# An offline order of 1,663 steps searched again, and every SBUF operand moved to a multiple of 128 bytes in its partition

## The chip, the core and the metric

The kernel runs on one core of one Trainium2 chip, in one launch. The metric is device time in microseconds, the median of several executions; lower is better. One profiled execution of the kernel before gives the rows below.

## The reference

Windowed attention, then two feed-forward blocks, all in float32:

```python
# q, k, v: 4 batches, 8 heads, 576 positions, 64 per head; window 64
attn = softmax(q @ k.T / 8 where 0 <= row - column < 64)      # rows sum to 1
x    = (attn @ v), heads side by side                          # 2304 x 512
h    = x @ w_in;  g = h * tanh(softplus(h)); x2 = g @ w_out    # 512 -> 2048 -> 512
h    = x2 @ w_in2                                              # 512 -> 1024
y    = h * softmax(h); z = (y - mean(y)) / sqrt(var(y) + 1e-6) * g_ln
out  = z @ w_out2                                              # 1024 -> 512
```

## The kernel before

Each float32 product is made of three TensorE passes over operands rounded to `fp32r` halves (`hi` and `lo`): hi·hi, hi·lo and lo·hi. The weights come as pairs of 32-bit words and are turned into float32 and then into halves on ACT and DVE. Tokens go in five groups of 512, 512, 512, 384 and 384.

The work has three stretches that overlap. Attention (`a_qk` to `a_xl`) makes `xt`, the halves of x, two blocks of 64 tokens at a time. The first feed-forward block (`pe_m1`, L950; `act_m`, L960; `g_h`, `g_l`; `pe_m2`, L984; `pe_m2l`, L995) runs over tiles of 128 hidden units. The second block works on tiles of 128 tokens: seven products of a Strassen-like scheme for `w_in2` (`b_p`, L1118), sums on DVE (`b_c`, L1133), softmax and norm (`b_max` to `b_z`), a transpose, and the last product (`b_m4`, L1235).

In `b_p` the stationary operand (`lhsT`) is `xs` for even pairs of token tiles and `xs_w` for odd pairs; the moving operand (`rhs`) is a half of `w_in2` in both. `xs` lies in a pool on the right side of SBUF, `xs_w` in the weights' pool on the left.

From attention block 16 on, and for every token tile of the second block, the transpose is not done on TensorE. DVE transposes blocks of 32 x 32 (`a_blocks`, L861; `b_tr`, L1200), one DMA writes them to DRAM (`blocks_out`, L375, tile `t_d`), and four DMAs read them back in the transposed order of blocks (`blocks_in`, L381). All DMAs are issued by SP, in program order.

The order of the instructions on every engine is not written out. `Schedule.run` simulates the kernel once while it is built: each step has a cost per engine, and of the steps that could start on an engine within `PATIENCE` (0.031 us) of the earliest, the one with the lowest entry in the list `RANK` is issued. `RANK` holds 1,663 numbers, found offline by a search over that same simulation. Behind a DMA step the simulation adds 1.6 us until what needs it may start, and 1.07 us between a step of another engine and a DMA that needs it. The costs are part of the program; the chip reads none of them, but they decide the order. Where the simulation foresees that TensorE idles in the first part, `bridge` issues matmuls of zeros (`zeros`, L693) to fill the time.

The rows of an SBUF tile begin where the pools before it end. On the left the pool `const` is first: `ident`, `mask_n` and `mask_0` of 512 bytes each per partition, starting at byte 1,152, then `g_sb` of 32 bytes; all other pools on the left follow, so each of their tiles (all halves of weights, `xt`, `g`, `lz`, `xs_w`) starts 32 bytes past a multiple of 128. The pools on the right are laid down from the top, which is such that `qk`, `v`, `s` and `xs` start 96 bytes past a multiple of 128.

Of the kernel before, what the change touches and what calls it, by code (L numbers as in the profile page):

```python
# [14 lines left out]
F32 = mybir.dt.float32  # L15
BF16 = mybir.dt.bfloat16
# [8 lines left out]
P = 128  # L25
# [4 lines left out]
N_T = 16  # L30
# [286 lines left out]
def attention_moe_solu(  # L317
# [46 lines left out]
    ident = const.tile([P, P], F32, name="ident")  # L364
    mask_n = const.tile([P, P], F32, name="mask_n")
    mask_0 = const.tile([P, P], F32, name="mask_0")
    g_sb = const.tile([P, NF2], F32, name="g_sb")

# [1298 lines left out]
```

## Time and profile before

| | us |
|---|---|
| median of 3 executions | 669.59 (665.54 to 669.97) |
| the profiled execution, its own time | 667.13 |
| span of its instructions | 665.4 |
| TensorE busy in the span | 649.1 (98%) |

The span runs from the first instruction to the last; the execution's own time has 1.7 us more around it. [...]

### The profile page before, as it was taken

The page shows a single profiled execution, that of the slowest core. Times are in us where ns is not written, and L with a number is a line of the kernel's source. Part 1 is how long each engine was busy: PE and PEld are TensorE (multiplying, and loading weights), DVE is VectorE, ACT ScalarE, POOL GpSimd, SP SyncE. Part 2 cuts the span into 40 slices and gives each one's busy share as a digit, 9 for nine tenths or more (in the row PEclk, how much of TensorE's full clock was granted, in tenths as well). Part 3 has the DMA queues.
Part 4 walks back from the last instruction along what each step waited for, and adds up shares of the span by engine and source line. Part 5 has one row for each costly group of instructions (what it writes and reads, how often), then busy time and mean ns, then how long its engine had stood idle before and what let it go on. Part 6 is the DMA issues. An engine that isn't in the chain of part 4 may idle for free.

```text
span 665.4 us, 10569 instructions
## 1 busy us (share of the span) xinstructions
PE 649.1 (98%) x4089; PEld 556.8 (84%) x4089; DVE 423.6 (64%) x741; ACT 348.3 (52%) x616; POOL 40.9 (6%) x63
## 2 busy tenths in 40 slices
PE   8899999999999989999999999999998999999997
PEld 6688888878888878788899999999886888788886
DVE  4778887876356656321115655776687988879751
ACT  5989775544344434232123545655576555657532
POOL 2412000000000001000000010000011001110100
PEclk9999999999999999999999999999999999999999
DMA  8874565576068453020044345602216555554562
GB/s 333 332 279 166 163 214 199 181 272 207 1 205 254 145 185 131 32 64 1 0 159 159 108 117 173 210 13 95 80 37 154 189 159 158 173 160 139 174 178 95
DMA packets 56962, 101.36 MB, mean 152 GB/s; under 512 B 5072, under 2 KB 30672, under 8 KB 56912
## 3 DMA queue, kind: packets, MB, share of 16 engines
q1 hardware_dynamic: 56912, 100.69, 46.5%
q8 instruction: 32, 0.52, 0.3%
q14 instruction: 18, 0.15, 0.1%
HBM read 74.45 MB, written 26.21 MB: 151 GB/s over the span
## 4 chain that ended last, share of the span: by engine, by line
PE 77%; DMA 10%; DVE 6%; ACT 3%; SPq 2%; issue 1%; POOL 0%; ACTq 0%; DVEq 0%
PE ps_h L950 26%; PE x L984 18%; PE po L1235 10%; PE x L995 9%; PE pb L1118 9%; DMA t_d<-s 3%; PE ps_o L903 2%; PE ps_s L741 2%; DMA h_b<-t_d 2%; DMA t_d<-y_b 2%; DMA st<-w_in 1%; SPq L381 1%; DMA room_q<-qk 1%; DMA pt<-t_d 1%; DMA xr<-x2d 1%
## 5 line engine op out<-in xcount | busy, mean ns | idle before, releaser
L950 PE MATMUL ps_h<-xt,w 128*128 128x512 f32 (+2 forms) x1008 | 205.4, 359 | 1.2 <-ACT mc L960 1.0
L950 PEld LDWEIGHTS ps_h<-xt,w 128*128 128x128 f32 x1008 | 177.2, 188 | 23.1 <-ACT mc L960 1.9
L984 PE MATMUL x<-g,w 128*128 128x512 f32 (+2 forms) x672 | 146.5, 359 | 1.0 <-DVE g L427 0.6
L984 PEld LDWEIGHTS x<-g,w 128*128 128x128 f32 x672 | 118.8, 188 | 16.3 <-ACT g L423 1.1
L443 DVE SCALAR_TENSOR_TENSOR g<-mc,g 128x512 fp32r<-128x512 f32 (+2 forms) x84 | 51.5, 618 | 94.8 <-ACT g L423 94.3
L1235 PE MATMUL po<-w,lz 128*128 128x512 f32 x432 | 101.4, 391 | 2.6 <-ACT lz L1215 2.5
L1235 PEld LDWEIGHTS po<-w,lz 128*128 128x128 f32 x432 | 80.6, 188 | 21.4 <-ACT lz L1215 4.6
L960 ACT ACTIVATE mc<-ps_h 128x512 f32<-128x512 f32 (+2 forms) x84 | 44.8, 535 | 98.5 <-PE ps_h L950 94.5
L995 PE MATMUL x<-g,w 128*128 128x512 f32 (+2 forms) x336 | 80.8, 362 | 0.0
L423 ACT ACTIVATE g<-mc 128x512 fp32r<-128x512 f32 (+2 forms) x68 | 39.2, 578 | 60.4 <-PE x L995 59.3
L995 PEld LDWEIGHTS x<-g,w 128*128 128x128 f32 x336 | 59.4, 188 | 7.9 <-issue 1.0
L1118 PE MATMUL pb<-w,xs 128*128 128x512 f32 x210 | 51.1, 395 | 0.0
L1118 PEld LDWEIGHTS pb<-w,xs 128*128 128x128 f32 x210 | 39.4, 188 | 9.2
L1118 PE MATMUL pb<-w,xs_w 128*128 128x512 f32 x168 | 39.8, 390 | 0.0
L1118 PEld LDWEIGHTS pb<-w,xs_w 128*128 128x128 f32 x168 | 31.5, 188 | 6.7
L1215 ACT ACTIVATE lz<-h_b 128x512 fp32r<-128x512 f32 x36 | 21.3, 626 | 29.6 <-DMA h_b<-t_d 19.4
L1219 DVE TENSOR_TENSOR lz<-h_b,lz 128x512 fp32r<-128x512 f32 x36 | 24.0, 686 | 17.3 <-ACT lz L1215 17.2
L508 DVE SCALAR_TENSOR_TENSOR st<-st 128x1024 uint32<-128x1024 uint32 x22 | 26.9, 1224 | 10.8 <-ACT st L493 9.2
L844 POOL TENSOR_TENSOR s<-s,rs 128x1024 f32<-128x1024 f32 x6 | 11.5, 1923 | 354.0 <-DMA x2d<-xs 187.3
L435 ACT ACTIVATE v_b<-pb 128x512 f32<-128x512 f32 x33 | 19.6, 595 | 20.0 <-PE pb L1118 18.2
L500 ACT ACTIVATE st<-st 128x1024 uint32<-128x1024 uint32 x22 | 25.4, 1156 | 6.3 <-DMA st<-w_out 6.3
L1150 ACT ACTIVATE e<-h_b,nm 128x1024 f32<-128x1024 f32 x18 | 20.7, 1151 | 9.1 <-DVE nm L1141 8.9
(133 smaller groups left out, 712.5 us busy)
## 6 DMA issues: line engine op xcount, KB each, us to landing
qk<-qk SPq DMA_DIRECT2D x32, 512.0 KB, 5.2
st<-w_out SPq DMA_DIRECT2D x12, 1024.0 KB, 5.7
st<-w_in SPq DMA_DIRECT2D x10, 1024.0 KB, 6.0
t_d<-y_b SPq DMA_DIRECT2D x18, 512.0 KB, 2.8
h_b<-t_d SPq DMA_DIRECT2D x72, 128.0 KB, 3.2
v<-v SPq DMA_DIRECT2D x32, 256.0 KB, 3.7
t_d<-s SPq DMA_DIRECT2D x10, 512.0 KB, 3.3
pt<-t_d SPq DMA_DIRECT2D x40, 128.0 KB, 3.1
```

Of the source, the lines that this page charges most:

```text
L423: nc.scalar.activation(out=hi, in_=x, func=ACTF.Copy, scale=1.0 if g is None else g)
L443: nc.vector.scalar_tensor_tensor(out=lo, in0=x, scalar=1.0 if g is None else g, in1=hi.bitcast(F32), op0=ALU.mult, op1=ALU.subtract)
L500: nc.scalar.activation(out=w, in_=w, func=ACTF.Copy, scale=0.9325 * 2.0**-29)
L508: nc.vector.scalar_tensor_tensor(out=lw, in0=uw, scalar=3, in1=lw, op0=ALU.logical_shift_left, op1=ALU.bitwise_or)
L950: nc.tensor.matmul(out=ps[:, :n], lhsT=w[:, a, k, fs], rhs=x[:, b, k, a0:a1], start=(idx == 0), stop=(idx == len(terms) - 1),)
L960: nc.scalar.activation(out=c[:, :n], in_=ht.pop(i)[:, :n], func=ACTF.Mish)
L984: nc.tensor.matmul(out=acc[j][m][:, a0:a1], lhsT=w[:, a, f % 4, m * P:(m + 1) * P], rhs=g[:, 0, :n], start=(i in opens and a == 0), stop=F ...
L995: nc.tensor.matmul(out=acc[j][m][:, a0:a1], lhsT=w[:, 0, f % 4, m * P:(m + 1) * P], rhs=g[:, 1, :n], start=False, stop=i in closes,)
L1118: nc.tensor.matmul(out=ps, lhsT=x[:, a, ix, k, :], rhs=w[:, k, :], start=first and n == 0, stop=n == len(terms) - 1, skip_group_check=not ...
L1215: nc.scalar.activation(out=lt[t][:, 0, fs].rearrange(SPLIT, i=4), in_=pst[t][:, :, fs], func=ACTF.Copy)
L1219: nc.vector.tensor_tensor(out=lt[t][:, 1, fs].rearrange(SPLIT, i=4), in0=pst[t][:, :, fs], in1=lt[t][:, 0, fs].bitcast(F32).rearrange(SPLI ...
L1235: nc.tensor.matmul(out=po[t], lhsT=lz[:, a, f, :], rhs=wt["w4", f // 4][:, b, f % 4, :], start=(c == 0 and idx == 0), stop=(c == 2 and idx ...
```

## The change

- `RANK` is replaced as a whole by another list, and twelve of the costs that the simulation uses are changed, up or down.
- `g_sb` leaves the pool `const` and gets a pool of its own behind the pools `st`, `x` and `m`; a pool `pad` of 96 bytes is laid down first on the right side. All operands of TensorE, and all other large tiles, then start at multiples of 128 bytes.
- The tile of zeros for `zeros` shrinks from 256 to 128 columns and is read twice as the moving operand; the matmuls stay 256 columns wide.

No operation is added or taken out; the order on every engine may differ.

```diff
 RANK = (
-    1391, 1126, 1485, 321, 317, 1647, 1410, 39, 308, 845, 739, 1366, 771, 176, 300, 796, 809, 70, 607, 668, 220, 44,
...
+    481, 441, 1200, 1017, 674, 1532, 1594, 90, 129, 446, 1432, 581, 510, 1398, 113, 784, 846, 1422, 1282, 1439, 29,
...
 )
...
-    g_sb = const.tile([P, NF2], F32, name="g_sb")
...
     m_p = actx.enter_context(tc.tile_pool(name="m", bufs=2))
+    g_p = actx.enter_context(tc.tile_pool(name="g_ln", bufs=1))
+    g_sb = g_p.tile([P, NF2], F32, name="g_sb")
...
+    pad = ctx.enter_context(tc.tile_pool(name="pad", bufs=1, side="right"))
+    pad.tile([P, 24], F32, name="pad")
...
-        w = sm_p.tile([P, 256], BF16, tag="warm", name="warm", bufs=1)
+        w = sm_p.tile([P, P], BF16, tag="warm", name="warm", bufs=1)
...
-            nc.tensor.matmul(out=ps[:, :256], lhsT=w[:, :P], rhs=w, start=True, stop=True)
+            nc.tensor.matmul(
+                out=ps[:, :256].rearrange("p (a b) -> p a b", a=2), lhsT=w, rhs=w.unsqueeze(1).to_broadcast([P, 2, P]),
+                start=True, stop=True,
+            )
...
-            r = step(dict(dve=0.35), t + offs[5], a_norm, n, after=[e1], new=[rs], uses=[nm, rs])
+            r = step(dict(dve=0.4), t + offs[5], a_norm, n, after=[e1], new=[rs], uses=[nm, rs])
...
-                sc = step(dict(dve=1.23 if n < N_T else 1.55), t + offs[1], a_scale, n, after=[qk, masks, mask_x] + moved[-1:], new=[s], uses=[S, s])
+                sc = step(dict(dve=1.23 if n < N_T else 1.42), t + offs[1], a_scale, n, after=[qk, masks, mask_x] + moved[-1:], new=[s], uses=[S, s])
...
-                bl = step(dict(dve=1.13), t + offs[7], a_blocks, n, after=[mu], uses=[s])
+                bl = step(dict(dve=1.25), t + offs[7], a_blocks, n, after=[mu], uses=[s])
...
-                mo = step(dict(dma=1.4), t + offs[8], a_out, n, after=[bl], new=[td, T], uses=[s, td])
-                c0 = step(dict(dma=2.0), t + offs[8], a_in, n, after=[mo], uses=[T, td])
+                mo = step(dict(dma=1.5), t + offs[8], a_out, n, after=[bl], new=[td, T], uses=[s, td])
+                c0 = step(dict(dma=2.6), t + offs[8], a_in, n, after=[mo], uses=[T, td])
...
-                q = step(dict(pe=1.362), a + P_AT[3], b_p, u, i, after=after, new=[bk[bank]] if first else [], uses=[bk[bank], xs_])
+                q = step(dict(pe=1.4), a + P_AT[3], b_p, u, i, after=after, new=[bk[bank]] if first else [], uses=[bk[bank], xs_])
...
-                    dict(dve=0.84), a + P_AT[5], b_c, u, i, c, after=after + [ob2], new=[hb[t]] if c == 0 else [],
+                    dict(dve=0.72), a + P_AT[5], b_c, u, i, c, after=after + [ob2], new=[hb[t]] if c == 0 else [],
...
-            sh = step(dict(dve=0.3), o[3], b_shift, t, after=[va], uses=[st])
+            sh = step(dict(dve=0.2), o[3], b_shift, t, after=[va], uses=[st])
...
-            tr = step(dict(dve=1.13), o[4], b_tr, t, after=[z, ob2], new=[Y], uses=[h, Y])
+            tr = step(dict(dve=1.25), o[4], b_tr, t, after=[z, ob2], new=[Y], uses=[h, Y])
...
-            mo = step(dict(dma=1.4), o[4], b_out_t, t, after=[tr], new=[td], uses=[Y, td])
-            mv = step(dict(dma=2.0), o[4], b_in_t, t, after=[mo], uses=[h, td])
+            mo = step(dict(dma=1.5), o[4], b_out_t, t, after=[tr], new=[td], uses=[Y, td])
+            mv = step(dict(dma=2.6), o[4], b_in_t, t, after=[mo], uses=[h, td])
```

## Rows read from the trace of the kernel before

**Rows 1.** The page's busy times and granted clock: us, share of the span, instructions.
```profile
PE 649.1 (98%) x4089; PEld 556.8 (84%) x4089; DVE 423.6 (64%) x741; ACT 348.3 (52%) x616; POOL 40.9 (6%) x63
...
PEclk9999999999999999999999999999999999999999
```
**Rows 2.** The page's chain that ended last, by engine.
```profile
PE 77%; DMA 10%; DVE 6%; ACT 3%; SPq 2%; issue 1%; POOL 0%; ACTq 0%; DVEq 0%
```
**Rows 3.** Stretches: length, PE, PEld, DVE, ACT, POOL busy; clock, DMA, GB/s.
```profile
0.00:20.00 20.00, 16.67 (x172) 13.10 (x172) 9.93 (x27) 12.65 (x59) 6.28 (x19) 1.00 0.92 343
...
200.00:250.00 50.00, 47.85 (x373) 39.12 (x372) 30.03 (x45) 20.25 (x26) 0.00 (x0) 1.00 0.62 195
...
500.00:550.00 50.00, 48.30 (x211) 38.88 (x210) 42.21 (x103) 29.23 (x52) 5.49 (x10) 1.00 0.58 163
550.00:600.00 50.00, 49.13 (x215) 39.85 (x214) 41.43 (x97) 29.30 (x54) 7.01 (x12) 1.00 0.51 159
```
**Rows 4.** TensorE's groups on `fp32r` halves: count, busy us, mean ns, idle before.
```profile
L950 PE MATMUL ps_h<-xt,w 128*128 128x512 f32 (+2 forms) x1008 | 205.4, 359 | 1.2 <-ACT mc L960 1.0
L984 PE MATMUL x<-g,w 128*128 128x512 f32 (+2 forms) x672 | 146.5, 359 | 1.0 <-DVE g L427 0.6 <-ACT g L423 0.4
L1235 PE MATMUL po<-w,lz 128*128 128x512 f32 x432 | 101.4, 391 | 2.6 <-ACT lz L1215 2.5
L995 PE MATMUL x<-g,w 128*128 128x512 f32 (+2 forms) x336 | 80.8, 362 | 0.0
L1118 PE MATMUL pb<-w,xs 128*128 128x512 f32 x210 | 51.1, 395 | 0.0
L1118 PE MATMUL pb<-w,xs_w 128*128 128x512 f32 x168 | 39.8, 390 | 0.0
```
**Rows 5.** TensorE's timeline, 531 to 546 us: start, length, first to last of a run.
```profile
531.24 11.04 PE L1235 MATMUL po<-w,lz 128*128 128x512 f32 x48
542.12 4.37 PE L1118 MATMUL pb<-w,xs 128*128 128x512 f32 x18
546.32 5.65 PE L1235 MATMUL po<-w,lz 128*128 128x512 f32 x24
```
**Rows 6.** Pieces of the chain on TensorE: start us, us, line, matmuls.
```profile
14.76 1.36 PE ps_s L693 x11
...
39.79 1.44 PE ps_h L950 x12
...
126.72 8.16 PE ps_h L950 x36
...
412.20 12.48 PE ps_h L950 x72
```
**Rows 7.** The group of the zeros between: their mean is the length of one.
```profile
L693 PE MATMUL ps_s<-warm 128*128 128x256 bf16 x20 | 2.5, 272 | 3.2 <-ACT s L435 1.6 <-ACT s L771 1.5
```
**Rows 8.** The chain around a block transpose of attention, 234 to 247 us.
```profile
234.55 1.16 DVE s L861
235.71 0.02 issue
235.72 5.79 DMA t_d<-s
...
242.85 3.10 DMA pt<-t_d
245.95 0.14 issue
246.09 1.15 PE ps_o L903 x32
```
**Rows 9.** The same of the second block, 556 to 567 us.
```profile
556.33 1.16 DVE y_b L1200
557.51 2.69 DMA t_d<-y_b
...
561.56 4.27 DMA h_b<-t_d
565.93 0.64 ACT lz L1215
566.61 3.48 PE po L1235 x14
```
**Rows 10.** The DVE transposes of blocks, by form.
```profile
L1200 DVE STREAM_TRANSPOSE y_b<-h_b 128x1024 f32<-128x1024 f32 x18 | 22.2, 1236 | 0.0
```
**Rows 11.** The first 100 us of L950, L984 and L995: PE, PEld, clock, DMA, GB/s.
```profile
0.00:100.00 100.00, 30.89 (x171) 25.82 (x172) 1.00 0.71 248
...
0.00:100.00 100.00, 17.25 (x96) 14.13 (x96) 1.00 0.71 248
...
0.00:100.00 100.00, 9.73 (x48) 7.31 (x48) 1.00 0.71 248
```

More of the change, by code (lines that the diff above doesn't have):

```diff
@@ L1420, in attend @@
                 sm = step(dict(dve=1.2), t + offs[5], a_sum, n, after=[ex], uses=[s])
-            r = step(dict(dve=0.35), t + offs[5], a_norm, n, after=[sm], new=[rs], uses=[rs])
+            r = step(dict(dve=0.4), t + offs[5], a_norm, n, after=[sm], new=[rs], uses=[rs])
             mu = step(COSTS["mul"], t + offs[6], a_mul, n, after=[r], uses=[s, rs], two=True)
```

158 rows, old and new, of the table RANK are left out of this document.

## The prediction

> **What bounds the kernel now.** I read the page's busy times first, then its chain, then TensorE's own spacing, then the stretches in which TensorE stands still. [...]
>
> That spacing is steady. 36 matmuls of 512 columns on `fp32r` halves take 8.16 us, 226.7 ns each; 72 of 384 take 12.48 us, 173.3 ns; 12 of 256 take 1.44 us, 120 ns [rows 6]. [...]
>
> One group is slower still. From 531.24 to 542.12 us 48 matmuls of `po` take 226.7 ns each; the next 18, whose stationary operand is `xs`, take 4.20 us, 233.3 ns; then `po` again [rows 5]. `xs_w` runs the same products from the left side. By the allocation, `xs` starts 96 bytes past a multiple of 128 and all the others 32, with the same kind of moving operand. So where an operand starts can matter: 6.6 ns per matmul between 96 and 32. What 0 gives, no row shows.
>
> **The change part by part.** The sum is made against the profiled execution's own 667.1 us (span 665.4 and 1.7 around it); the median of the runs shown is 669.6, 2.5 us more.
>
> *`xs` on a multiple of 128.* 210 matmuls [rows 4] at 6.6 ns is 1.4 us, if 0 is as good as 32. They lie in the last 180 us, where TensorE is the chain for most of the time, so I count all of it: -1.4 us. Left out if the place of `xs` is not the cause.
>
> *All other `fp32r` matmuls from 32 to 0.* They are 1008 + 672 + 432 + 336 + 168 = 2616 [rows 4]. [...] At worst 0 costs what 96 costs, +6.6 ns each, +17.3 us. I take 0. [...]
>
> [...]
>
> *The order.* TensorE's idle time that a changed cost can reach is where it waits for block transposes. From the end of the DVE transpose at 235.71 us to the product at 246.09 are 10.4 us [rows 8], and from 557.51 to 565.93 in the second block 8.4 us [rows 9]. The simulation before reckons 1.07 + 1.4 + 1.6 + 2.0 + 1.6 = 7.7 us for this way, the new one 1.07 + 1.5 + 1.6 + 2.6 + 1.6 = 8.4; the transpose itself goes from 1.13 to 1.25, where the trace has 1.24 [rows 10]. So the new order should start these ways about 0.8 us sooner, or put other matmuls in between. TensorE stands still 2.15 us in 200 to 250, 1.70 in 500 to 550 and 0.87 in 550 to 600 [rows 3]: 4.7 us. Moved 0.8 us sooner, the wait of 0.87 goes and the longer ones shrink; with something gained from sums that the old costs of `b_c` and `b_shift` made too long, I count -3 us. Bounds: -4.7 us, and +4, since the search knows neither the 10.4 us nor the slow reads beside full DMA queues and can put as much waiting elsewhere. The 3.3 us of idle time in the first 20 us [rows 3] sit beside DMAs at 92% and stay. The later pieces of a moved step go with it: a transpose moved forward takes five issues on SP with it, and SP's other loads stand behind them; loads are issued well ahead in the stretches from 200 us on, so I price that at nothing, and if it were not so the wait would be of the size of the +4. The cost 1.4 for `b_p` is a little too high if `xs` gets faster (63 steps by 0.04 us, 2.4 us over the last part); the order then has matmuls that end sooner than it thinks, which costs at most short waits on DVE.
>
> *The rest.* The zeros keep their 256 columns; `g_sb` is read by the same instructions; the smaller `memset` ends before the first loads have landed. Nothing.
>
> Sum: 667.1 - 1.4 - 0 - 3 = **662.7 us**; its own range, from the bounds of the order and of `xs`, is 658 to 669.
>
> **The rivals.**
>
> [...]
>
> [...] A stationary offset of 96 costs 6.6 ns more than 32; if 0 saves as much again, it is 2616 x 6.6 = 17.3 us and 210 x 13.2 = 2.8: 667.1 - 20.1 - 3 = 644 us, and up to 655 where the step is smaller (half of it, 3.3 ns).
>
> *The change does not do what it says.* The place of `xs` is not the cause (then all 210 stay at 233), and the new order's waits take the place of the old ones: 667 us, 664 to 671.
>
> *Slower.* 0 is as bad as 96: every `fp32r` matmul has the spacing that the rows of `xs` show, 233.3 ns for 512 columns. 667.1 + 17.3 - 3 = 681 us. It decides from the point where the loss passes 1% and what the order gives: (6.7 + 3) us / 2616 = 3.7 ns per matmul, all through the kernel. For it: offsets do matter in the trace. Against it: it needs 0 to be worse than 32, while 96 is worse than 32.
>
> **How the numbers follow.** Forecast 0.45, stream 0.22, half 0.15, no effect 0.10, slower 0.08. The predicted time is the forecast's, 662.7. To hold 8 in 10 the range reaches over the two fast rivals, down to 635, and up to 669; left out are the slower rival and some of the stream's and the no-effect case's spread. A measurement of this kernel tells about 1% from no change. Faster by over 1%: 0.22 + 0.15, and a quarter of the forecast where the order gives its upper bound, 0.48. Slower by over 1%: 0.08 and a little for a bad order, 0.09. Within 1%: 0.43.
>
> **What would show it.** [...] If `xs` stays at 233 while all start at multiples of 128, its place was not the cause. The idle time of TensorE in the two stretches after 200 us should fall from 4.7 to about 2 us; if it is as large at other places, the order gave nothing. I am wrong above all if the spacing of the 2616 changes.

## The result and the profile after

| | before | after |
|---|---|---|
| median, us | 668.49 (664.76 to 669.97, 6 runs) | 658.22 (656.25 to 659.02, 6 runs) |
| the profiled execution, us | 667.13 | 659.02 |
| span, us | 665.4 | 657.2 |

The ratio after to before is 0.9853, 95% interval 0.983 to 0.9875: 9.8 us less. The forecast of 662.7 was 4.4 us below the profiled execution of before; after's is 8.1 below it. The page of after, busy times, granted clock and chain, answers to [rows 1, 2]:

```profile
PE 645.9 (98%) x4080; PEld 556.7 (85%) x4080; DVE 424.3 (65%) x741; ACT 347.4 (53%) x617; POOL 47.7 (7%) x62
...
PEclk9899999999999999999999999999999999999999
...
PE 85%; DMA 8%; DVE 2%; ACT 1%; SPq 1%; issue 1%; POOL 0%; ACTq 0%
```

The span is 8.2 us shorter. Span less busy time is TensorE's standstill: 665.4 - 649.1 = 16.3 before, 657.2 - 645.9 = 11.3 after, 5.0 us less. The other 3.2 us are less busy time. Its groups, to be held against [rows 4]:

```profile
L1242 PE MATMUL po<-w,lz 128*128 128x512 f32 x432 | 100.8, 389 | 0.2 <-ACT lz L1222 0.2
...
L1125 PE MATMUL pb<-w,xs 128*128 128x512 f32 x210 | 49.9, 389 | 0.0
```

`xs` has lost 1.2 us of 51.1 and its matmuls now last as long as those of `po`; `po` has lost 0.6 of 101.4. Nine matmuls are gone (4089 to 4080): all are zeros, 59 before and 50 after, 1.0 us at (1360 - 272) / 10 = 108.8 ns from start to start [rows 6, 7]. The stretches that answer to [rows 3], with the same columns:

```profile
0.00:20.00 20.00, 16.38 (x174) 12.57 (x174) 11.60 (x28) 13.51 (x62) 9.17 (x20) 1.00 0.93 341
200.00:250.00 50.00, 48.84 (x387) 39.87 (x380) 31.04 (x47) 20.80 (x27) 0.00 (x0) 1.00 0.63 198
500.00:550.00 50.00, 49.76 (x219) 40.51 (x218) 44.63 (x109) 32.47 (x57) 8.11 (x10) 1.00 0.52 164
550.00:600.00 50.00, 50.00 (x222) 41.44 (x221) 43.35 (x105) 29.59 (x50) 11.69 (x14) 1.00 0.48 153
```

TensorE's standstill in the last three is 1.16, 0.24 and 0 us, where it was 2.15, 1.70 and 0.87. The chain around a block transpose of attention, then the first of the second block, against [rows 8, 9]:

```profile
216.71 4.08 DMA t_d<-s
222.13 5.25 DMA pt<-t_d
227.62 1.15 PE ps_o L910 x32
...
493.32 2.73 DMA t_d<-y_b
500.25 4.93 DMA h_b<-t_d
506.30 11.20 PE po L1242 x48
```

The second of the two DVE transposes there, from the timeline:

```profile
494.03 1.24 DVE L1207 STREAM_TRANSPOSE y_b<-h_b 128x1024 f32<-128x1024 f32 x1
```

The ways have not become shorter. From the first DMA's issue to the product it is 227.62 - 216.71 = 10.9 us in attention. In the second block the chain passes from one token tile to another on SP: the write at 493.32 us is the first tile's, while the product at 506.30 us reads the second tile's `lz`, whose transpose ended at 494.03 + 1.24 = 495.27. Its way is thus 11.0 us, where [rows 9] has 566.61 - 557.51 = 9.1. What is new is what TensorE has to do meanwhile: it works on other products, takes the second tile first, and waits 0.24 us for those 11.0.

### The profile page after: what moved, and what is told of

It is laid out like the page before. It is cut to its first block, busy times and chain, and to the rows that moved or that the text cites. A ratio compares the mean times of both kernels' runs of the same rounds, so it can differ in the third digit from the quotient of the medians.

```text
span 657.2 us, 10526 instructions
## 1 busy us (share of the span) xinstructions
PE 645.9 (98%) x4080; PEld 556.7 (85%) x4080; DVE 424.3 (65%) x741; ACT 347.4 (53%) x617; POOL 47.7 (7%) x62
## 4 chain that ended last, share of the span: by engine, by line
PE 85%; DMA 8%; DVE 2%; ACT 1%; SPq 1%; issue 1%; POOL 0%; ACTq 0%
PE ps_h L957 27%; PE x L991 17%; PE po L1242 15%; PE pb L1125 10%; PE x L1002 9%; PE ps_o L910 3%; DMA st<-w_out 2%; PE ps_s L748 2%; DMA room_q<-qk 1%; DMA st<-w_in 1%; PE ps_t L863 1%; DMA qk<-qk 1%; DMA pt<-t_d 1%; DMA h_b<-t_d 1%; SPq L380 1%
## 5 line engine op out<-in xcount | busy, mean ns | idle before, releaser
L1242 PE MATMUL po<-w,lz 128*128 128x512 f32 x432 | 100.8, 389 | 0.2 <-ACT lz L1222 0.2
L1125 PE MATMUL pb<-w,xs 128*128 128x512 f32 x210 | 49.9, 389 | 0.0
L1188 POOL TENSOR_SCALAR va<-va 128x1 f32<-128x1 f32 x18 | 12.2, 677 | 423.2 <-PE pb L1125 308.6
L1125 PE MATMUL pb<-w,xs_w 128*128 128x512 f32 x168 | 40.2, 390 | 0.0
L512 DVE SCALAR_TENSOR_TENSOR st<-st 128x1024 uint32<-128x1024 uint32 x22 | 28.5, 1297 | 10.9 <-ACT st L504 8.9
L1249 ACT ACTIVATE o<-po 128x512 f32<-128x512 f32 x18 | 10.7, 597 | 30.6 <-PE po L1242 17.1
L497 ACT ACTIVATE st<-st 128x1024 f32<-128x1024 f32 x18 | 20.7, 1151 | 11.5 <-DMA st<-w_in 9.8
```

Of the source, the lines that this page charges most:

```text
L497: nc.scalar.activation(out=w, in_=w, func=ACTF.Copy, scale=2.0**-112)
L512: nc.vector.scalar_tensor_tensor(out=lw, in0=uw, scalar=3, in1=lw, op0=ALU.logical_shift_left, op1=ALU.bitwise_or)
L1125: nc.tensor.matmul(out=ps, lhsT=x[:, a, ix, k, :], rhs=w[:, k, :], start=first and n == 0, stop=n == len(terms) - 1, skip_group_check=not ...
L1242: nc.tensor.matmul(out=po[t], lhsT=lz[:, a, f, :], rhs=wt["w4", f // 4][:, b, f % 4, :], start=(c == 0 and idx == 0), stop=(c == 2 and idx ...
```

## The experiments

**Layout alone, order alone.** One kernel has the layout part of the change (the smaller tile of zeros with it) and the list and costs of before; the other has the new list and costs with the layout of before.

```diff
-    g_sb = const.tile([P, NF2], F32, name="g_sb")
...
+    g_sb = g_p.tile([P, NF2], F32, name="g_sb")
...
+    pad.tile([P, 24], F32, name="pad")
```

> The kernel before with the new layout alone; its order and costs stay. Theory (the place of xs was the whole of the layout's part, the order the rest): xs falls from 233.3 to 226.7 ns, all other fp32r matmuls stay at 226.7, 173.3 and 120; 210 x 6.6 = 1.4 us less than before, ratio 0.998. Rival (aligned operands help elsewhere too, in transfers, DVE or ACT): 4 us or more less than before, ratio 0.994 or lower.

> The changed kernel with the layout of before: new list, new costs, old places. Theory: xs back at 233.3 ns; 1.4 us over the changed kernel's 658.2, so 659.6, ratio to before 0.987; TensorE idle as in the changed kernel, some 11 us. Rival (the layout carries more than xs): 662 or more, ratio over 0.990.

Layout alone: 665.37 us, ratio 0.9962 (0.994 to 0.9983). Order alone: 658.56 us, ratio 0.988 (0.9852 to 0.9909). Of the whole, then, some 2.5 us (1.1 to 4.0) are the layout's, and 7 to 8 the order's: 0.9853 / 0.9962 = 0.989 with the new layout, 0.988 with the old one. The profiled span of layout alone is 664.0, 1.4 us below before, and its `xs` group has 49.8 us. TensorE's stretches with the order alone (length, busy, clock, DMA, GB/s):

```profile
0.00:100.00 100.00, 94.72 (x943) 1.00 0.73 258
100.00:200.00 100.00, 99.96 (x601) 1.00 0.52 173
200.00:250.00 50.00, 49.77 (x382) 1.00 0.65 201
...
500.00:550.00 50.00, 50.00 (x220) 1.00 0.51 158
550.00:600.00 50.00, 50.00 (x220) 1.00 0.50 157
```

From 100 us to its last matmul TensorE hardly stops any more: 0.27 us in place of 5.1. In the first 100 us it stands still 5.28 us in place of 7.44.

**Is it the multiple of 128?** Five kernels keep the new order and move the left side, `xs`, or both. The distance below counts from the start of the moving half of the weight to the start of `xs`, within 256 bytes; in the kernel before it is 64.

```diff
+    const.tile([P, 24], F32, name="pad_l")
...
-    pad.tile([P, 24], F32, name="pad")
```

> The changed kernel with every operand 96 bytes past a multiple of 128, left and right. Theory A (what counts is how far the stationary operand's start stands from the moving one's within 128 bytes): all at 226.7 ns, xs too, and the time of the changed kernel, 658. Theory B (what counts is the start of the operand itself, and 96 is a slow place): 233 ns for 512 columns everywhere, 2826 x 6.6 = 18.7 us more, 677.

Here all operands start 96 bytes past a multiple of 128, as `xs` alone did before. The other four have a pad of 64 bytes on the left, or 32, 64 or 224 in place of 96 bytes on the right.

```diff
+    const.tile([P, 16], F32, name="pad_l")
```

> The changed kernel with all tiles of the left side 64 bytes past a multiple of 128 and xs on one. Theory A (distance of the two starts): xs at about 233 ns, since its weights stand 64 bytes away as they did before; all others at 226.7; 1.4 us over the changed kernel, 660. Theory B (own start): xs at 226.7 or less, the others between 226.7 and 233, so up to 9 us more, 660 to 667.

```diff
-    pad.tile([P, 24], F32, name="pad")
+    pad.tile([P, 8], F32, name="pad")
```

> The changed kernel with the left side on multiples of 128 and xs 64 bytes past one. Theory A (distance): xs at 233 ns as before, since the distance is 64 as before; others 226.7; 660. Theory B (own start, worse the further it stands from the multiple): xs between 226.7 and 233, some 230 ns; 659.

```diff
-    pad.tile([P, 24], F32, name="pad")
+    pad.tile([P, 56], F32, name="pad")
```

> The changed kernel with xs 128 bytes further down, still on a multiple of 128 but at a distance of 128 instead of 0 within 256 bytes from its moving operand. If 128 bytes are the unit, xs stays at 226.7 ns and the time at 658; if the unit is 256 bytes, xs is slower, like the 228.9 and 233.3 ns of the distances 192 and 64, and the time 0.5 to 1.4 us longer.

```diff
-    pad.tile([P, 24], F32, name="pad")
+    pad.tile([P, 16], F32, name="pad")
```

> The changed kernel with xs 32 bytes ahead of its moving operands. Theory A (distance within 256 bytes): between the 226.7 ns of 0 and the 233.3 ns of 64, so 227 to 233, and 658 to 660. Rival (own start): 226.7, since 32 was a fast place before.

The order is the same in all, so the same two runs of `xs` can be read from TensorE's timeline: one of 42 matmuls and one of 6. After:

```profile
487.89 9.68 PE L1125 MATMUL pb<-w,xs 128*128 128x512 f32 x42
...
540.91 1.52 PE L1125 MATMUL pb<-w,xs 128*128 128x512 f32 x6
```

The same place for `xs_w`, in the kernel after too:

```profile
478.37 9.68 PE L1125 MATMUL pb<-w,xs_w 128*128 128x512 f32 x42
```

All at 96:

```profile
486.27 9.68 PE L1124 MATMUL pb<-w,xs 128*128 128x512 f32 x42
...
539.28 1.52 PE L1124 MATMUL pb<-w,xs 128*128 128x512 f32 x6
```

64 on the left, `xs` on a multiple of 128:

```profile
485.57 9.78 PE L1126 MATMUL pb<-w,xs 128*128 128x512 f32 x42
...
538.23 1.54 PE L1126 MATMUL pb<-w,xs 128*128 128x512 f32 x6
```

All on multiples of 128, but `xs` 128 bytes further:

```profile
486.11 9.92 PE L1125 MATMUL pb<-w,xs 128*128 128x512 f32 x42
...
539.06 1.56 PE L1125 MATMUL pb<-w,xs 128*128 128x512 f32 x6
```

`xs` at 64, and at 32 (9.96 and 1.56 in both):

```profile
488.21 9.96 PE L1125 MATMUL pb<-w,xs 128*128 128x512 f32 x42
...
541.64 1.56 PE L1125 MATMUL pb<-w,xs 128*128 128x512 f32 x6
```

In these views a matmul lasts longer than it is to the start of the next (389 ns in the mean for `xs` in after), so that two in a row overlap. The difference of two runs leaves out the last one's length, and divided by 36 it is the time from start to start, the spacing: (9.68 - 1.52) / 36 = 226.7 ns, and so on.

| layout | distance within 256 | spacing of `xs`, ns | us |
|---|---|---|---|
| after | 0 | 226.7 | 658.22 (6 runs) |
| all at 96 | 0 | 226.7 | 657.72 (2) |
| `xs` at 32 | 32 | 233.3 | 659.83 (1) |
| `xs` at 64 | 64 | 233.3 | 660.62 (1) |
| `xs` 128 further | 128 | 232.2 | 657.89 (1) |
| left at 64 | 192 | 228.9 | 656.59 (1) |

A multiple of 128 is not needed (all at 96 is as fast as after; ratio to before 0.9841, 0.9812 to 0.9869) and not enough (128 further is on a multiple and slow). In these kernels it went by whether both operands of a matmul start at the same place within 256 bytes: 226.7 ns where they do, 228.9 to 233.3 where they don't. With 64 on the left `xs` stands where it stands in after, and yet is slower, so that its own place is not the cause. The unit is not 512 either: by the allocation `xs` stands 256 of 512 bytes from its moving operand in after and `xs_w` 0, and both have 9.68 us for 42. The times of single runs can't rank layouts whose whole effect is 1.4 us; the spacings can. The expectation that took 128 as the unit fell with the kernel at 128, and 64 on the left gave 228.9 ns where it said 233.

**The same for the other operands.** 128 unused bytes ahead of the pool of `xt` and `g` put these moving operands 128 bytes from their stationary weights. All start on multiples of 128, as after.

```diff
     st_p = actx.enter_context(tc.tile_pool(name="st", bufs=2))
+    gap = actx.enter_context(tc.tile_pool(name="gap", bufs=1))
+    gap.tile([P, 32], F32, name="gap")
     x_p = actx.enter_context(tc.tile_pool(name="x", bufs=2))
```

> The changed kernel with 128 unused bytes laid ahead of xt and g: every operand is still on a multiple of 128, but the moving operands of the first feed-forward block now stand 128 bytes from their stationary ones within 256. Theory A (the distance of the two starts within 256 bytes sets the spacing, on any tile): the 2016 matmuls of that block go from 226.7, 173.3 and 120 ns to some 6 ns more, as xs did with a distance of 128 (232.6 ns); 12 us more, 670; po and pb unchanged. Rival (only the place of xs on the right side is slow): all as in the changed kernel, 658.

664.18 us, ratio 0.9938 (0.9916 to 0.996), 6 us slower than after. The timeline of this kernel, 512 and then 384 columns:

```profile
125.65 5.73 PE L959 MATMUL ps_h<-xt,w 128*128 128x512 f32 x24
...
136.81 14.09 PE L959 MATMUL ps_h<-xt,w 128*128 128x512 f32 x60
...
415.37 4.38 PE L959 MATMUL ps_h<-xt,w 128*128 128x384 f32 x24
...
421.69 12.80 PE L959 MATMUL ps_h<-xt,w 128*128 128x384 f32 x72
```

And of after:

```profile
125.08 5.60 PE L957 MATMUL ps_h<-xt,w 128*128 128x512 f32 x24
...
135.96 13.76 PE L957 MATMUL ps_h<-xt,w 128*128 128x512 f32 x60
...
410.54 4.32 PE L957 MATMUL ps_h<-xt,w 128*128 128x384 f32 x24
...
416.78 12.64 PE L957 MATMUL ps_h<-xt,w 128*128 128x384 f32 x72
```

512 columns: (14.09 - 5.73) / 36 = 232.2 ns against 226.7; 384 columns: 8.42 / 48 = 175.4 against 173.3. So the distance matters for the matmuls of the first block too, and costs 5.5 ns at 512 columns and 2.1 at 384. Twice as much time was expected, as if each of the 2016 paid alike. The groups of `ps_h` and `x` grow by 3.4 + 2.5 + 1.2 = 7.1 us of busy time. By these prices 1056 matmuls of 512 columns and 768 of 384 would make 5.8 + 1.6 = 7.4 us (an estimate), so that the 192 of 256 columns show none; `po` and `pb`, which were not moved, keep 100.8, 49.9 and 40.2.

**Where the order gains: early, late, or both.** Two kernels with the new layout run a fixed list of steps: those that start before 340 us in the simulation of one order, then the rest in the other's.

```diff
-            s.key = RANK[n]
...
+        seq = list(zip(SEQ, ENG))
...
+            for n, (s, e) in enumerate(todo):
```

> The changed layout; the steps that the simulation starts before 340 us in the new order, the rest in the order of before. TensorE idle before 340 us should be as with the new order (some 5.5 us), behind it as with the old one (3 us). Theory C (the gain of the order lies where TensorE stood waiting, 2.2 us in the first 100, 1.9 in 200 to 250, 3 behind 340, each worth its idle time): 665.4 of the layout alone less 4.1 to 5, 661. Rival D (the first part's gain is swallowed later, only the second block's part counts): 664 to 665.

> The reverse: the old order before 340 us, the new one behind it, changed layout. Theory C: 665.4 less the 3 us of waits behind 340 us and about 1 us of slower restarts after them, 661.5; both halves together then make up the order's 7 to 8 us. Rival D: all of the order's gain lies here, 658 to 659.

New early: 662.52 us, 0.9913 (0.9887 to 0.9938). New late: 663.06 us, 0.9929 (0.9909 to 0.9949). Against layout alone (0.9962) that is -3.3 and -2.2 us, each good to some 2 us by the intervals, and together 5.5 of the 7.3 that the whole new order gives there. TensorE's stretches in layout alone:

```profile
200.00:250.00 50.00, 47.86 (x373) 1.00 0.61 192
500.00:550.00 50.00, 48.04 (x205) 0.97 0.56 167
```

New early:

```profile
200.00:250.00 50.00, 50.00 (x389) 1.00 0.67 200
...
500.00:550.00 50.00, 48.50 (x214) 1.00 0.51 155
550.00:600.00 50.00, 48.41 (x214) 1.00 0.53 173
```

New late:

```profile
200.00:250.00 50.00, 47.71 (x372) 1.00 0.60 192
...
500.00:550.00 50.00, 48.91 (x214) 1.00 0.52 159
550.00:600.00 50.00, 50.00 (x222) 1.00 0.47 148
```

Layout alone stands still 2.14 us in 200 to 250 and 1.99 in 500 to 600. New early removes the first and has 3.09 in the second; new late keeps 2.29 in the first and has 1.09 in the second. Each half thus shortens the standstill of its own stretches only: the gain is not one event, and of what is removed early at most 1.1 us is given back late. The missing 1.8 us sit where the halves are joined, or within the intervals; which, these runs don't tell.

**Was it the way of the block transposes?** Layout alone, old order, but the DMAs of the second block's token tiles write and read only the first 64 of 256 elements.

```diff
-        nc.sync.dma_start(out=d.rearrange("i a b x -> (i a) b x"), in_=src.rearrange("p b h c -> p b (h c)"))
+        w = 64 if isinstance(key, tuple) else 256
+        nc.sync.dma_start(out=d.rearrange("i a b x -> (i a) b x")[:, :, :w], in_=src.rearrange("p b h c -> p b (h c)")[:, :, :w])
...
```

> The order of before with the changed layout; the transposes of the token tiles write and read only the first 64 of each 256 elements, so that the output is not the reference's. Theory (the old order's waits in the second block come from a way of the transposes that is longer than it reckoned): if the way gets shorter by 0.8 us or more, TensorE's idle time in 500 to 600 us falls from 2.0 to under 0.5 us, and the time by 2 us against the layout alone, to 663. Rival (the waits come from DVE being late, not from the way): the idle time stays near 2 us and the time at 665.

661.92 us, 0.9918 (0.9891 to 0.9944): 2.9 us below layout alone. The DMA issues of layout alone (count, KB, us from issue to landing):

```profile
t_d<-y_b SPq DMA_DIRECT2D x18, 512.0 KB, 2.9
h_b<-t_d SPq DMA_DIRECT2D x72, 128.0 KB, 3.0
```

And of the short way:

```profile
t_d<-y_b SPq DMA_DIRECT2D x18, 128.0 KB, 2.3
h_b<-t_d SPq DMA_DIRECT2D x72, 32.0 KB, 1.9
```

The way is 1.7 us shorter, and the stop in the second block goes with it. Layout alone, TensorE's timeline, then its stretches of 2 us:

```profile
506.94 9.18 PE L1242 MATMUL po<-w,lz 128*128 128x512 f32 x32 [1.96 <-ACT lz L1222]
...
508.00:510.00 2.00, 2.00 (x7) 0.60 0.37 80
510.00:512.00 2.00, 2.00 (x6) 0.55 0.00 0
```

The short way:

```profile
506.86 7.49 PE L1244 MATMUL po<-w,lz 128*128 128x512 f32 x32
```

So the old order's late waits were for this way, as the prediction had it. This kernel shortens the landing and relieves the DMA queues at once; the two weren't told apart.

**New costs with the old list.**

```diff
-                c0 = step(dict(dma=2.0), t + offs[8], a_in, n, after=[mo], uses=[T, td])
+                c0 = step(dict(dma=2.6), t + offs[8], a_in, n, after=[mo], uses=[T, td])
```

This and the other eleven costs; `RANK` stays.

> The changed kernel with the list of before under the new costs. Theory (the list's numbers mean nothing without the costs that they were searched with): the kernel's own simulation ends at 692.5 us in place of 652.1, so some 40 us more than the changed kernel, 695 to 705. Rival (the corrected costs alone carry the gain, whatever the list): 657 to 663.

710.35 us in one run, above the 695 to 705 that were expected. The page's busy times:

```profile
PE 672.9 (95%) x4253; PEld 575.9 (81%) x4253; DVE 421.3 (59%) x738; ACT 349.9 (49%) x617; POOL 39.0 (5%) x62
```

TensorE stands still 708.5 - 672.9 = 35.6 us, and 4253 - 4089 = 164 more zeros are issued than before. The list breaks ties of one particular simulation. With other costs other steps meet, and the same numbers give an order that nobody searched for.

Was the new list better, or the costs truer? By its own reckoning the new order gains nothing: the simulation of before ends at 652.1 us with the old costs, and that of after at 652.1 us with the new ones. The chip's span is 13.3 us longer than that before and 5.1 us after. This speaks for the costs; but it is one list for each, and no other list found with the old costs was run.

## Why the prediction was right, and where its sum was not

**`xs`, -1.4 us: right.** 210 matmuls went from 233.3 to 226.7 ns, and layout alone shortened the profiled span by 1.4 us; the medians say 1.1 to 4.0, so that nothing here shows more from the layout than `xs`. (The matmuls lie from 464 to 629 us, not all in the last 180.) The cause named was not exact: not the start within 128 bytes, but the distance of the two operands within 256. The change met it because, by the allocation, `xs` and the weights both came to 128 within 256.

**All others from 32 to 0, taken as 0, at worst +17.3: right.** 226.7 and 173.3 ns before and after. Both operands of these matmuls stood, and stand, at the same offset. In all at 96 nothing but the common offset differs, and the spacing is the same to 0.1 ns. With that the two fast rivals fall (stream and half in the chances, the second at 644 us): a misaligned start cost nothing by itself (common starts 0, 32, 64 and 96 bytes past a multiple of 128 all give 226.7 ns), and no run shows a shorter spacing for 512 columns. The slower rival's 233.3 ns came near what was measured elsewhere, but its condition was wrong: it needs operands that stand apart, as in the kernel with the gap (232.2 ns there, +6 us for the matmuls of the first block). What the runs show is that for `fp32r` at 512 columns the place of one operand against the other costs up to 6.6 ns: 226.7 at a distance of 0, 233.3 at 64, 232.2 at 128.

**What the spacing is made of stays open.** The 120, 173.3 and 226.7 ns of [rows 6] for 256, 384 and 512 columns are 53.3 ns for each 128 columns and 13.3 ns beside, the same at all three widths. The price of the distance is not the same: 5.5 ns at 512 columns and 2.1 at 384. The two are different things, and what the 13.3 ns are, no run here settled.

**The order, -3 us between -4.7 and +4: mis-sized.** It measured -7 to -8. The account from views, before to order alone: behind 100 us the standstill fell by 4.8 us (5.1 to 0.27); in the first 100 us by 2.2 (7.44 to 5.28); nine zeros fewer, 1.0 us. That is 8.0 of the 8.9 by which the two spans differ; the rest is in single groups by tenths. Two steps failed. The lower bound took all of the idle time in three stretches, yet I counted 3 of 4.7, as if the long waits could only shrink by the 0.8 us that the costs were wrong; the new order doesn't move the same wait by 0.8 us, it puts other matmuls there (the 11.0 us way above, with 0.24 us of waiting). And I said that the idle time of the first 20 us stays, which is nearly so (3.33 to 2.75 in the order alone), but read no stretch from 20 to 80 us. There TensorE stood still 4.1 us before and 2.5 in the order alone, most of the early gain.

**The total: inside the range in part by luck.** With `xs` at 1.4 us and the order at its bound of 4.7 the lowest sum is 667.1 - 6.1 = 661.0; the 658 of the forecast's own range needs 3.7 us for `xs`. No run shows that term; the runs show 1.4 us in its place. The wide range reached down to 635 for two rivals that fell, and no run shows the faster spacing that they need. The 658.2 is there because the order gave more than its bound.

**A part of the stops that was not in the sum.** In layout alone a stop cost more than its length: 1.96 us of standstill ahead of 506.94 are followed by a granted clock of 0.60 and 0.55 over 4 us, and the 32 matmuls take 9.18 us where the short way, without the stop, has 7.49: 1.7 us, nearly as much as the stop. That execution shows it and the profiled one of before, with waits of 1.9 and 1.7 us and a granted clock of 1.00 behind both, does not; so it is in some executions only. Beside the experiments 29 of 55 executions of before have a mean granted clock of 0.997 or less over the whole core, 6 of 12 of layout alone, 4 of 10 of new early, but 1 of 10 of new late and 1 of 6 each of order alone and after; the 29 of before take 1.7 us longer in the mean than the other 26. This suggests that the new late order avoids some of these places too. The profile of before has none of them, so that its span can't show this part; the medians hold it. After's own profile has such a place early, TensorE's stretches:

```profile
20.00:22.00 2.00, 1.75 (x21) 0.75 1.06 406
22.00:24.00 2.00, 2.00 (x21) 0.50 1.03 411
24.00:26.00 2.00, 2.00 (x27) 0.89 1.03 400
```

What the granted clock lacks there, 0.25, 0.50 and 0.11 of 2 us each, is 1.7 us, in an execution that is 659.02 and the highest of its six; the profile of all at 96, without such a place, has a span of 655.6.

**The rest, nothing: right.** The zeros keep their 272 ns (that there are nine fewer comes with the order), and no wait has `g_sb` or the zeros' tile at its end beyond the 1.0 us on the tile's `memset` that stood before as well.

**"Does not do what it says": fell,** on both counts: `xs` is at 226.7, and the new order's waits are fewer, not moved. No version here is clearly better than after; all at 96 and 64 on the left lie within its spread.

## What to carry to other kernels

Before padding for alignment, look at which two operands meet in a matmul and compare their starts with each other, over 256 bytes and not 128 (here a distance of 128 cost 5.5 ns of 226.7); the steady spacing of long runs, taken as a difference of two runs, shows in one profile what the total time hides. When an offline order is searched again with truer costs, look at the idle time in every stretch of the profile, and not only at the error of the cost: here nearly all of it behind 100 us went, and some before. Costs and the list found under them are one object: change neither alone.

## What the runs showed of the hardware

- The spacing of `fp32r` matmuls with 512 columns depended on the distance of the two operands' starts within 256 bytes: 226.7 ns at 0, 233.3 at 32 and 64, 232.2 at 128, 228.9 at 192. It did not go by each start's own alignment: with all at 96 it was 226.7 too.
- At a distance of 128, with the moving operand 128 bytes further, 512 columns paid 5.5 ns, 384 columns 2.1, and 256 columns nothing that shows: at these two prices the other widths make 7.4 us (an estimate), and 7.1 were measured.
- In layout alone a standstill of 1.96 us was followed by a granted clock of 0.60 and 0.55 from 508 to 512 us, at a price of 1.7 us (32 matmuls in 9.18 us in place of 7.49). In after two waits of 0.88 and 0.94 us close together were followed by 0.75, 0.50 and 0.89 from 20 to 26 us; behind waits of 1.9 and 1.7 us in before it stayed at 1.00.
